# A transformer block on one core: the seam between attention and MLP is put in another order (first MLP unit, last output product, row preparation, one load)

## The chip, the core and the metric

The kernel runs on one core of a Trainium2 chip. The core has five engines with an instruction queue each, worked off in order: TensorE (PE in the profile; its weight loads are PEld), VectorE (DVE), ScalarE (ACT), GpSimd (POOL) and SyncE (SP, which here only issues DMAs; ACT and POOL issue DMAs too). An instruction waits on semaphores for what other engines or DMAs must have finished first. The metric is the time of one execution on the device, in microseconds (us).

## The reference

A pre-norm transformer block over 2048 rows of 576 numbers, 32 heads of 18, then a gated MLP of width 4608:

```python
def _layernorm(x, axis=-1, eps=1e-5):
    m = jnp.mean(x, axis=axis, keepdims=True)
    v = jnp.var(x, axis=axis, keepdims=True)
    return (x - m) / jnp.sqrt(v + eps)
...
    x = A_x
    h = x + _A_ref(_layernorm(x, axis=-1), A_wqkv, A_wo)
    h2 = h + _B_ref(_layernorm(h, axis=-1), B_w_gate, B_w_up, B_w_down)
    return h2
```

`_A_ref` is softmax attention followed by the product with wo (the output product); `_B_ref` is `(gelu(h @ w_gate) * (h @ w_up)) @ w_down`. Inputs and output are f32.

## The kernel before

**Rows and stages.** The 2048 rows are four blocks of 512 (`NB = 4`), each of four tiles of 128 rows (`TPB = 4`). The residual stream lies in `nat`, 16 tiles of 128 x 576. The program is one long list per engine, written out by Python generators: a *main* generator emits the TensorE work piece by piece, and at each of its `yield`s one step of a *side* generator is emitted (`beside`, `take`). So the order on every engine is the order in which the Python code runs; nothing reorders it later.

**Attention, then the output product.** The last head group's attention ends with `out_block` (L593 to L641): it normalizes 128 x 512 numbers and writes them with small DMAs into `XT` (tile name X), the transposed operand of the output product. For the last block, four of these DMAs are issued from ScalarE's queue (L637, L639). `wo_block(b)` (L681) computes the output product of a block: 8 halves of a row tile, 14 matmuls each (L694, shown as L279), each evacuated by VectorE with the residual added (L695), then row statistics (L699) and, at the end, 13 small VectorE operations for the inverse deviation (`rstd_of`, L700). The residual tiles are fetched from x into two buffers (L685).

**The MLP.** The blocks are taken in two pairs (p = 0: blocks 0 and 1, p = 1: blocks 2 and 3), and each pair's 2 x 2 block product is done with 7 products in place of 8, after the scheme of Strassen and Winograd, in f16 high and low parts. So the rows of a pair must first be normalized, combined (T1 to T4), split into high and low parts and transposed: that is `pair_rows` (L713). `rows0()` does it for pair 0 inside the last attention stage, `rows1()` for pair 1. Per row tile (4 of them): two norms on VectorE (L723, L724, shown as L215), four GpSimd subtractions (L726 to L729), three casts on ScalarE (`high`, shown as L732), nine VectorE operations for the low parts (L734 to L736), and five DMA transposes (L749): the one for pieces 9 to 17 is issued on ScalarE's queue, the other four on SyncE's.

**A unit and a down product.** `unit(c, p)` (L895) is one chunk of 256 MLP columns for one pair: 14 products of 7 matmuls (L909), one per `yield`, numbered 1 to 14 below. Banks are shared between products, so a product waits until ScalarE or VectorE has read what its bank held: product 11 adds to the bank that the copy at L955 reads after product 9, product 12 to the one that L959 reads after product 10. Gates are `gate` (L917), casts `high(i, j)` (L920), low parts `low(i, j)` on GpSimd (L923). `down(p)` (L986) is 16 groups of 12 matmuls (L998, shown as L279) that read those high and low parts; VectorE adds each to `nat` (L999). The steady state from L1113 on takes, per two chunks, `unit(c, 1)`, `unit(c+1, 1)`, `down(1)`, `unit(c+2, 0)`, `unit(c+3, 0)`, `down(0)`; the side steps load and split the next weights (`split_matrix`, `split_down`). Both need the largest magnitude of a weight matrix: VectorE reduces it (L127, L131), TensorE transposes the result (L136), VectorE makes a scale of it (L140 to L171), ScalarE then cuts the high parts (L825, L881, L885).

**The seam** (L1073 to L1112). After the last attention step: 8 products of `unit(0, 0)`, with two steps of `out_block` among them (after 2 and after 5 products); then `wo_block(3)`; then products 9 to 14 of `unit(0, 0)`; then `unit(1, 0)`; then `down(0)`, with two side steps per group; then what is left of the side steps; then `load_matrix(w_gate, 2)` on SyncE's queue, and the steady state begins with `unit(0, 1)`, the first unit that reads pair 1's rows.

Of the kernel before, what the change touches and what calls it, by code (L numbers as in the profile page):

```python
# [11 lines left out]
F16 = mybir.dt.float16  # L12
# [6 lines left out]
P = 128  # L19
# [12 lines left out]
def tile_block(  # L32
# [645 lines left out]
    xbs = [view(A, MAT, (D,)), view(WK, 19968, (D,))]  # L678
    PIECES = 2 * NK + 9

    def wo_block(b, ring_):  # L681

        def fetch(t):
            if t < (b + 1) * TPB:
                nc.sync.dma_start(xbs[t % 2], xv[:, t])  # L685

        fetch(b * TPB)
        fetch(b * TPB + 1)
        yield
# [23 lines left out]
    def pair_rows(p, F, T4, parts, high):  # L713

        b12, B22, B11, B21, T1, T2, T3 = (F[:, i] for i in range(7))
        y2, y1 = (F.rearrange("p a b -> p (a b)")[:, i * D : (i + 1) * D] for i in range(2))
        M2, M3 = 2 * P, 3 * P
        for rows in parts:
            nc.gpsimd.memset(rows[:, :, M3 - KR : M3], 0.0)
        jobs = ((0, 4, F[:, 1:5]), (4, 6, F[:, 5:7]), (6, 7, T4.unsqueeze(1)))  # L720
        for i in range(TPB):
            t1, t2 = 2 * p * TPB + i, (2 * p + 1) * TPB + i
            normed(y1, nat[:, t1], t1)  # L723
            normed(y2, nat[:, t2], t2)  # L724
            yield
            nc.gpsimd.tensor_sub(T1, b12, B11)  # L726
            nc.gpsimd.tensor_sub(T2, B22, T1)
            nc.gpsimd.tensor_sub(T4, B21, T2)
            nc.gpsimd.tensor_sub(T3, B22, b12)  # L729
            yield  # L730
            for (o0, o1, f), r in zip(jobs, parts):
                high(r[:, :, :HALF], f)  # L732
                yield
                nc.vector.tensor_sub(r[:, :, M3:], f[:, :, :M2], r[:, :, :M2])  # L734
                nc.vector.tensor_sub(r[:, :, HALF : HALF + KR], f[:, :, M2:], r[:, :, M2:HALF])
                nc.vector.tensor_copy(r[:, :, HALF + KR : HALF + 2 * KR], r[:, :, M2:HALF])  # L736
                k0, k1 = 5 * o0, 5 * o1
                flat = r.rearrange("p a b -> p (a b)")
                for a, b in ((0, 9), (9, 18), (18, 35)):
                    a, b = max(a, k0), min(b, k1)  # L740
                    if a >= b:
                        continue
                    if a < 18:
                        o = (2 * p + a // 9) * TB + i * P
                        dst = XT[:, a % 9 : a % 9 + b - a, o : o + P]
                    else:
                        v = p * PIECES + a - 18
                        dst = VP[:, v : v + b - a, i * P : (i + 1) * P]
                    (turn_on[a % 2] if p else nc.sync).dma_start_transpose(dst, flat[:, (a - k0) * P : (b - k0) * P])  # L749
                yield  # L750


# [3 lines left out]
    def rows0():  # L756
# [2 lines left out]
            view(V, o + 8064 + 1280 * a, (n, 5 * P), F16) for a, n in ((0, 4), (4, 2), (6, 1))],  # L759
            nc.vector.tensor_copy)  # L760

    def rows1():
        return pair_rows(1, view(A, MAT, (7, HALF)), T4s, [
            view(A, MAT + 8064, (4, 5 * P), F16), view(V, 36864, (2, 5 * P), F16),
            view(A, MAT + 8064 + 5120, (1, 5 * P), F16)], nc.scalar.copy)


    S1, S2, S3, S4, A12, A22, A11, A21 = range(8)
    B22, B11, B21, T1, T2, T3, T4 = range(7)
# [125 lines left out]
    def unit(c, p):  # L895

        gsc, hsc = scales[c % 2]
        hh, hl = hts[c % 2]
        g, u = ([b[:, :TB] for b in banks[3 * i : 3 * i + 3]] for i in range(2))

        def product(m, bank, a, b, start):
            wh, wl = slots[c % 2][m]
            ks = [piece(p, 5 * b + k) for k in range(5)]
            mm = []
            for k in range(2):
                mm += [(wh[:, a, k], ks[k]), (wh[:, a, k], ks[3 + k]), (wl[:, a, k], ks[k])]
            mm += [(wh[:, a, 2], ks[2])]
            for i, (w, x_) in enumerate(mm):
                nc.tensor.matmul(bank, w, x_, start=start and i == 0,  # L909
                                 stop=i == len(mm) - 1,  # L910
                                 skip_group_check=not start)

        def gelu(dst, src_):
            nc.scalar.activation(dst, src_, AF.Gelu_apprx_tanh, scale=gsc)

        def gate(dst, v):
            nc.vector.scalar_tensor_tensor(dst, v, hsc, dst, op0=ALU.mult, op1=ALU.mult)  # L917

        def high(i, j, v):
            nc.scalar.copy(hh[:, 2 * i + j], v)  # L920

        def low(i, j, v):
            nc.gpsimd.tensor_sub(hl[:, 2 * i + j], v, hh[:, 2 * i + j])  # L923
# [22 lines left out]
        nc.scalar.copy(au, u[0])  # L946
# [8 lines left out]
        nc.scalar.copy(bg, g[0])  # L955
# [12 lines left out]
        yield  # L968
        product(1, u[0], A22, T4, False)
        low(1, 1, bg)  # L970
        gate(ga, u[0])
        yield
        product(0, g[2], S4, B22, False)
        high(1, 0, ga)
        nc.vector.tensor_add(ag, g[2], ag)
        gelu(ag, ag)
        low(1, 0, ga)
        yield
        product(1, u[2], S4, B22, False)
# [50 lines left out]
    for n in range(NS):  # L1030
# [3 lines left out]
        for kt in range(NT):  # L1034
# [33 lines left out]
            if n == NS - 2 and kt == NT // 2:  # L1068
# [12 lines left out]
    tmps += [view(V, 2 * 2 * PIECES * TB, (TB,)), view(WK, 19968, (TB,)), view(W, 33792, (TB,), F32)]  # L1081
# [6 lines left out]
    it = unit(0, 0)  # L1088
    side = chain(second, pause(5), split_matrix(1, 1, None, lambda: load_down(0, nc.gpsimd), 2),
                 pause(5), split_down(0), rows1())  # L1090

    def beside(main, side, n=1, more=0, head=0):

        for i, _ in enumerate(main):
            if i >= head:
                take(side, n + (i % 3 == 2) * more)

    beside(islice(it, 2), side)
    take(ob)
    beside(islice(it, 3), side)  # L1100
    take(ob)
    beside(islice(it, 3), side)
    beside(wo_block(NB - 1, m_ring), side)
    beside(it, side, 1, 1)
    beside(unit(1, 0), side, 1, 1)
    while not dscs:
        take(side)
    beside(down(0, dscs[-1], NCH == 2), side, 2, head=0)
    run(side)
    blank_rows()  # L1110
    load_matrix(w_gate, 2)
    tmps.append(view(A, MAT, (TB,)))  # L1112
    for sc in range(NCH // 2):  # L1113
        c = 2 * sc
# [2 lines left out]
        if not last:  # L1117
# [49 lines left out]
```

## Time and profile before

| what | value |
|---|---|
| median of 3 runs | 2811.88 us (2808.3 to 2812.98) |
| the profiled execution | 2811.68 us, span 2809.9 us |
| granted TensorE clock, mean | 0.989 |
| busy: PE, DVE, ACT, POOL | 94%, 78%, 54%, 24% of the span |
| last attention matmul | 1547 us |
| `unit(0, 1)` starts, ends | 1666.29, 1694.32 us |

All times inside the execution are counted from the start of the span. In a row of the timeline the columns are start, duration, engine, line, operation, output <- input, count of merged instructions, and in brackets the idle time of the engine just before them with what ended it. A matmul's duration includes its pipeline; the step from one start to the next is what it costs. PEclk is the TensorE clock that the throttle granted.

### The profile page before, as it was taken

The page shows a single profiled execution, that of the slowest core. Times are in us where ns is not written, and L with a number is a line of the kernel's source. Part 1 is how long each engine was busy: PE and PEld are TensorE (multiplying, and loading weights), DVE is VectorE, ACT ScalarE, POOL GpSimd, SP SyncE. Part 2 cuts the span into 40 slices and gives each one's busy share as a digit, 9 for nine tenths or more (in the row PEclk, how much of TensorE's full clock was granted, in tenths as well). Part 3 has the DMA queues.
Part 4 walks back from the last instruction along what each step waited for, and adds up shares of the span by engine and source line. Part 5 has one row for each costly group of instructions (what it writes and reads, how often), then busy time and mean ns, then how long its engine had stood idle before and what let it go on. Part 6 is the DMA issues. An engine that isn't in the chain of part 4 may idle for free. (4 is left out here: it accounts for less than half of the span.)

```text
span 2809.9 us, 43719 instructions
## 1 busy us (share of the span) xinstructions
PE 2643.0 (94%) x16665; PEld 1092.9 (39%) x16665; DVE 2179.0 (78%) x3950; ACT 1517.7 (54%) x1872; POOL 688.2 (24%) x833
## 2 busy tenths in 40 slices
PE   7899999999999999999997779999999999999999
PEld 3542222222222222222233445555555555555555
DVE  6379999999999999999979656575757575656563
ACT  5216877777777777777754324343334343333332
POOL 2101432211212122122215233232323222322221
PEclk9999999999999999999999999999999999999999
DMA  8311110000101010010014241010101010101011
GB/s 218 78 49 42 40 40 14 25 23 14 40 12 36 14 40 12 19 31 18 23 29 105 62 76 32 28 44 16 49 21 38 21 45 19 44 21 38 21 57 39
DMA packets 162823, 111.99 MB, mean 40 GB/s; under 512 B 82612, under 2 KB 141620, under 8 KB 162612
## 3 DMA queue, kind: packets, MB, share of 16 engines
q1 hardware_dynamic: 150479, 95.30, 12.3%
q0 software_dynamic: 7296, 12.66, 1.7%
q8 instruction: 130, 2.13, 0.3%
q10 hardware_dynamic: 4837, 1.25, 0.2%
q14 instruction: 81, 0.66, 0.1%
HBM read 74.45 MB, written 14.42 MB: 32 GB/s over the span
## 5 line engine op out<-in xcount | busy, mean ns | idle before, releaser
L535 DVE TENSOR_REDUCE mx<-bank 128x1 f32<-128x512 f32 x2048 | 1264.9, 682 | 30.0 <-PE bank L532 30.0
L581 ACT ACTIVATE WK<-pair 128x1024 f32<-128x1024 f32 x1024 | 991.4, 1021 | 301.2 <-PE pair L579 300.9
L585 PE MATMUL bank<-WK,V 128*32 128x512 f32 x4096 | 548.3, 607 | 0.2 <-ACT nat L599 0.2
L279 PEld LDWEIGHTS <-WK 128*128 128x128 f16 x3456 | 337.5, 98 | 109.6 <-issue 12.2
L909 PEld LDWEIGHTS <-W 128*128 128x128 f16 x2394 | 234.7, 98 | 284.5 <-issue 7.8
L532 PE MATMUL bank<-W 54*128 54x512 f16 x1024 | 291.4, 382 | 40.1 <-DVE mx L535 10.0
L532 PE MATMUL bank<-A 54*128 54x512 f16 x1024 | 279.8, 380 | 38.1 <-DVE mx L535 6.3
L585 PEld LDWEIGHTS bank<-WK,V 128*32 128x32 f32 x4096 | 81.0, 108 | 438.0 <-issue 410.5
L279 PE MATMUL bank<-W,WK 128*128 128x288 f16 x1728 | 236.6, 286 | 13.1 <-POOL WK L923 7.3
L279 PE MATMUL more<-W,WK 128*128 128x288 f16 x1728 | 235.2, 286 | 4.9 <-DVE nat L999 4.9
L608 POOL TENSOR_TENSOR rp<-rc,minus_one 128x16 f32<-128x16 f32 x28 | 81.8, 2922 | 615.1 <-DMA rc<-nat 615.1
L909 PE MATMUL more<-X,W 128*128 128x512 f16 x792 | 223.8, 379 | 0.0
L909 PE MATMUL more<-V,W 128*128 128x512 f16 x720 | 203.4, 380 | 1.7 <-ACT tmp L959 1.7
L809 POOL TENSOR_TENSOR A<-A 128x384 f32<-128x384 f32 x144 | 146.5, 1038 | 207.9 <-DMA A<-in_B_w_up_dram 119.8
L923 POOL TENSOR_TENSOR WK<-tmp,WK 128x512 f16<-128x512 f32 x73 | 89.9, 1231 | 332.9 <-ACT WK L920 324.5
L579 PE MATMUL pair<-W 56*128 56x512 f16 x1024 | 156.5, 378 | 3.6 <-ACT WK L581 2.8
L825 ACT ACTIVATE W<-A,p_s_m 128x768 f16<-128x768 f32 (+1 forms) x78 | 78.2, 1035 | 147.6 <-DVE p_s_m L171 147.4
L532 PEld LDWEIGHTS <-W 54*128 54x128 f16 x1024 | 59.7, 93 | 248.7 <-issue 220.3
L579 PE MATMUL pair<-A 56*128 56x512 f16 x1024 | 153.7, 375 | 0.2
L532 PEld LDWEIGHTS <-A 54*128 54x128 f16 x1024 | 57.2, 93 | 235.0 <-issue 204.1
L999 DVE SCALAR_TENSOR_TENSOR nat<-more,p_dsc,nat 128x288 f32<-128x288 f32 x144 | 74.4, 517 | 91.1 <-PE more L279 89.6
L927 ACT COPY tmp<-bank 128x512 f32<-128x512 f32 x36 | 20.9, 582 | 214.3 <-PE bank L909 190.6
(262 smaller groups left out, 2884.3 us busy)
## 6 DMA issues: line engine op xcount, KB each, us to landing
A<-in_B_w_down_dram SPq DMA_DIRECT2D x8, 1152.0 KB
nat<-rc SPq DMA_DIRECT2D x32, 256.0 KB
A<-in_B_w_gate_dram SPq DMA_DIRECT2D x64, 128.0 KB
A<-in_B_w_up_dram SPq DMA_DIRECT2D x64, 128.0 KB
qk_hi<-qk SPq DMA_DIRECT2D x36, 128.0 KB
qk_lo<-qk SPq DMA_DIRECT2D x36, 128.0 KB
out_dram<-nat SPq DMA_DIRECT2D x16, 288.0 KB
X<-nat SPq DMA_DIRECT2D x100, 36.0 KB
```

What stands on the lines that cost most here:

```text
L279: nc.tensor.matmul(dst, a, b, start=(i == 0), stop=(i == len(pairs) - 1))
L532: nc.tensor.matmul(pms[j][:, :TB], Q[r, q0 : q0 + P], K[r, kc * TB : (kc + 1) * TB], start=True, stop=True)
L535: nc.vector.tensor_reduce(mx[:, t, 2 * pr + j, kc : kc + 1], pms[j][:, :TB], axis=AX.X, op=ALU.max)
L579: nc.tensor.matmul(pS[:, j, :TB], K[r, kt * P : (kt + 1) * P], Q[r, qc * TB : (qc + 1) * TB], start=True, stop=True)
L581: nc.scalar.activation(pes[(2 * kt + pr) % NPE], pS[:, :, :TB], AF.Exp, scale=ex_reg)
L585: nc.tensor.matmul(acc[32 * hh : 32 * hh + 32, :TB], Vg[n // NB][:, kt * G4 + hh * VC : kt * G4 + hh * VC + 32], pes[(2 * kt + hh // 2) % ...
L608: nc.gpsimd.tensor_tensor(rc, den, minus_one.to_broadcast([P, R]), op=ALU.pow)
L809: op(W8[:, d], W8[:, a], W8[:, b])
L825: by = hi_on or (lambda dst, src, k: nc.scalar.activation(dst, src, AF.Copy, scale=k))
L909: nc.tensor.matmul(bank, w, x_, start=start and i == 0, stop=i == len(mm) - 1, skip_group_check=not start)
L923: nc.gpsimd.tensor_sub(hl[:, 2 * i + j], v, hh[:, 2 * i + j])
L999: nc.vector.scalar_tensor_tensor(nat[:, t, ws], pt[:, :HALF], dsc, nat[:, t, ws], op0=ALU.mult, op1=ALU.add)
```

## The change

1. `unit(0, 0)` runs whole (14 products) ahead of `wo_block(3)`, with the second step of `out_block` after 8 products in place of 5. The last output product takes its banks from the ring of four (`down_ring`) in place of two, and fetches its residual tiles into two buffers of the WK region; the two first fetches are issued before `unit(0, 0)`.
2. `rows1()` is written out anew: its two norms go from VectorE to ScalarE (`nc.scalar.activation` with Identity, scale and bias), and a row tile takes 5 or 4 side steps in place of 8. Its operations on GpSimd, its casts, its low parts and its five DMA transposes stay as they were, in the same order (`turn_rows` holds what was written in `pair_rows`).
3. The extra side steps (`more`, and two per group in `down(0)`) are gone: one side step per yield everywhere. One of the pauses is shorter by one.
4. `blank_rows()` and `load_matrix(w_gate, 2)` become the last side step (`first_load`), so SyncE issues them behind the last DMA transpose, inside `down(0)` rather than behind it. In the first `unit(0, 1)` the side steps begin after 7 products (`head=7`).
5. In every unit, `high(1, 0)` and `low(1, 0)` are emitted ahead of the yield between products 12 and 13, so ahead of that yield's side step; before they stood behind it.

```diff
-    def wo_block(b, ring_):
+    def wo_block(b, ring_, xbs=xbs):
...
     def rows1():
-        return pair_rows(1, view(A, MAT, (7, HALF)), T4s, [
-            view(A, MAT + 8064, (4, 5 * P), F16), view(V, 36864, (2, 5 * P), F16),
-            view(A, MAT + 8064 + 5120, (1, 5 * P), F16)], nc.scalar.copy)
...
+        def high(k):
+            nc.scalar.copy(parts[k][:, :, :HALF], jobs[k][2])
+
+        def low(k, i):
+            o0, o1, f = jobs[k]
+            r = parts[k]
+            nc.vector.tensor_sub(r[:, :, M3:], f[:, :, :M2], r[:, :, :M2])
+            nc.vector.tensor_sub(r[:, :, HALF : HALF + KR], f[:, :, M2:], r[:, :, M2:HALF])
+            nc.vector.tensor_copy(r[:, :, HALF + KR : HALF + 2 * KR], r[:, :, M2:HALF])
+            turn_rows(1, i, 5 * o0, 5 * o1, r)
+
+        for i in range(TPB):
+            t1, t2 = 2 * TPB + i, 3 * TPB + i
+            for y, t in ((y1, t1), (y2, t2)):
+                nc.scalar.activation(y, nat[:, t], AF.Identity, scale=rs[:, t : t + 1],
+                                     bias=nb[:, t : t + 1])
+            nc.gpsimd.tensor_sub(T1, b12, B11)
+            nc.gpsimd.tensor_sub(T2, B22, T1)
+            nc.gpsimd.tensor_sub(T4, B21, T2)
+            nc.gpsimd.tensor_sub(T3, B22, b12)
+            yield
+            high(0)
+            yield
+            low(0, i)
+            high(1)
+            high(2)
+            yield
+            low(1, i)
+            yield
+            low(2, i)
+            if i % 2 == 0:
+                yield
...
         gate(ga, u[0])
+        high(1, 0, ga)
+        low(1, 0, ga)
         yield
         product(0, g[2], S4, B22, False)
-        high(1, 0, ga)
         nc.vector.tensor_add(ag, g[2], ag)
         gelu(ag, ag)
-        low(1, 0, ga)
...
+    last_wo = wo_block(NB - 1, down_ring, [view(WK, 8192 + 4 * D * i, (D,)) for i in range(2)])
+    next(last_wo)
+
+    def first_load():
+        blank_rows()
+        load_matrix(w_gate, 2)
+        yield
+
     side = chain(second, pause(5), split_matrix(1, 1, None, lambda: load_down(0, nc.gpsimd), 2),
-                 pause(5), split_down(0), rows1())
+                 pause(4), split_down(0), rows1(), first_load())
...
-    beside(islice(it, 3), side)
+    beside(islice(it, 6), side)
     take(ob)
-    beside(islice(it, 3), side)
-    beside(wo_block(NB - 1, m_ring), side)
-    beside(it, side, 1, 1)
-    beside(unit(1, 0), side, 1, 1)
-    while not dscs:
-        take(side)
-    beside(down(0, dscs[-1], NCH == 2), side, 2, head=0)
+    beside(it, side)
+    beside(last_wo, side)
+    tmps[5] = view(W, 33792, (TB,), F32)
+    beside(unit(1, 0), side)
+    assert dscs
+    beside(down(0, dscs[-1], NCH == 2), side)
     run(side)
-    blank_rows()
-    load_matrix(w_gate, 2)
...
-        beside(unit(c, 1), side)
+        beside(unit(c, 1), side, head=0 if sc else 7)
```

ScalarE's queue at the seam, before, from the first cast of `unit(0, 0)` on (L639 are the four small DMAs of the last attention output; L946 is the copy behind product 6, L955 and L959 those behind products 9 and 10, L825 the cut of the weights for `unit(1, 0)`):

```order
L920 CAST WK<-tmp 128x512
L625 CAST nat<-nat 128x512
L639 DMA X<-nat 10x512
L639 DMA X<-nat 18x512 x3
L946 COPY V<-more_12734 128x512
L825 ACTIVATE W<-A,p_s_m_12964 128x1152
L825 ACTIVATE W<-A,p_s_m_12964 128x768 x2
L955 COPY WK<-bank_66 128x512
L959 COPY W<-more_12734 128x512
```

The same place now (L962 is the cast, L988, L997 and L1001 the three copies, L956 a gelu):

```order
L962 CAST WK<-tmp 128x512
L988 COPY V<-more_12734 128x512
L625 CAST nat<-nat 128x512
L639 DMA X<-nat 10x512
L639 DMA X<-nat 18x512 x3
L997 COPY WK<-bank_66 128x512
L1001 COPY WK<-more_12734 128x512
L956 ACTIVATE WK<-WK,p_gsc_12143 128x512
```

The copy behind product 6 now stands ahead of the four DMA issues; the copies behind products 9 and 10, which products 11 and 12 wait for, stand right behind them.

ScalarE's queue in `unit(1, 0)`, before, from the copy behind product 6 to the first gelu behind product 10 (L732 are casts of the rows of pair 1, L749 the DMA transpose):

```order
L946 COPY WK<-more_12734 128x512
L732 CAST A<-A 128x4x288
L955 COPY W<-bank_66 128x512
L749 DMA_TRANSPOSE X<-A 128x9x128
L732 CAST V<-A 128x2x288
L959 COPY tmp<-more_12734 128x512
L914 ACTIVATE W<-W,p_gsc_12803 128x512
```

Now, from the copy behind product 9 to the first DMA transpose (L791 are the norms of the first row tile, L778 its first cast):

```order
L997 COPY W<-bank_66 128x512
L1001 COPY tmp<-more_12734 128x512
L956 ACTIVATE W<-W,p_gsc_12805 128x512
L791 ACTIVATE A<-nat,nb,rs 128x576 x2
L956 ACTIVATE tmp<-bank_66,p_gsc_12805 128x512
L962 CAST WK<-W 128x512
L778 CAST A<-A 128x4x288
L962 CAST WK<-tmp 128x512
L763 DMA_TRANSPOSE X<-A 128x9x128
```

The rows of pair 1 begin later in the unit (behind product 10 in place of product 6), and no cast or transpose of theirs stands ahead of the copies behind products 9 and 10 any more.

ScalarE's queue at the end of `unit(1, 1)`, the last unit ahead of a `down(1)`, before (L825 is the cut of the next weights, the cast of tmp behind it is `high(1, 0)`):

```order
L920 CAST WK<-A 128x512
L825 ACTIVATE W<-A,p_s_m_13858 128x1152
L920 CAST WK<-tmp 128x512
L914 ACTIVATE WK<-WK,p_gsc_12803 128x512
L825 ACTIVATE W<-A,p_s_m_13858 128x768
```

And now:

```order
L962 CAST WK<-A 128x512
L962 CAST WK<-tmp 128x512
L867 ACTIVATE W<-A,p_s_m_13860 128x1152
L956 ACTIVATE WK<-WK,p_gsc_12805 128x512
L867 ACTIVATE W<-A,p_s_m_13860 128x768
```

The two have changed places, in each of the eight `unit(c+1, 1)` that have a weight to cut; no other row of ScalarE's queue differs from there to the end.

More of the change, by code (lines that the diff above doesn't have):

```diff
@@ L736, in pair_rows @@
                 nc.vector.tensor_copy(r[:, :, HALF + KR : HALF + 2 * KR], r[:, :, M2:HALF])
[L737 to L749, printed above, removed]
+                turn_rows(p, i, 5 * o0, 5 * o1, r)
                 yield
@@ L760, in rows0, with turn_rows @@
             nc.vector.tensor_copy)
-    def rows1():
-        return pair_rows(1, view(A, MAT, (7, HALF)), T4s, [
-            view(A, MAT + 8064, (4, 5 * P), F16), view(V, 36864, (2, 5 * P), F16),
-            view(A, MAT + 8064 + 5120, (1, 5 * P), F16)], nc.scalar.copy)
+    def turn_rows(p, i, k0, k1, rows):
+        flat = rows.rearrange("p a b -> p (a b)")
+        for a, b in ((0, 9), (9, 18), (18, 35)):
+            a, b = max(a, k0), min(b, k1)
+            if a >= b:
+                continue
+            if a < 18:
+                o = (2 * p + a // 9) * TB + i * P
+                dst = XT[:, a % 9 : a % 9 + b - a, o : o + P]
+            else:
+                v = p * PIECES + a - 18
+                dst = VP[:, v : v + b - a, i * P : (i + 1) * P]
+            (turn_on[a % 2] if p else nc.sync).dma_start_transpose(dst, flat[:, (a - k0) * P : (b - k0) * P])
@@ new lines, in rows1 @@
+    def rows1():
+        F, T4 = view(A, MAT, (7, HALF)), T4s
+        parts = [view(A, MAT + 8064, (4, 5 * P), F16), view(V, 36864, (2, 5 * P), F16),
+                 view(A, MAT + 8064 + 5120, (1, 5 * P), F16)]
+        b12, B22, B11, B21, T1, T2, T3 = (F[:, i] for i in range(7))
+        y2, y1 = (F.rearrange("p a b -> p (a b)")[:, i * D : (i + 1) * D] for i in range(2))
+        M2, M3 = 2 * P, 3 * P
+        for rows in parts:
+            nc.gpsimd.memset(rows[:, :, M3 - KR : M3], 0.0)
+        jobs = ((0, 4, F[:, 1:5]), (4, 6, F[:, 5:7]), (6, 7, T4.unsqueeze(1)))
+        def high(k):
[28 more added lines that the diff above has]
+                yield
@@ L1080, in tile_block @@
     tmps += [small.tile([P, TB], F32, tag="tmp", name="tmp", bufs=3) for _ in range(3)]
-    tmps += [view(V, 2 * 2 * PIECES * TB, (TB,)), view(WK, 19968, (TB,)), view(W, 33792, (TB,), F32)]
+    tmps += [view(V, 2 * 2 * PIECES * TB, (TB,)), view(WK, 19968, (TB,)), view(WK, 8192 + 8 * D, (TB,))]
     pairs_in.close()
@@ L1087, in tile_block, with beside @@
     down_ring = ring([singles[0], more[0], singles[1], more[1]])
-    it = unit(0, 0)
+    last_wo = wo_block(NB - 1, down_ring, [view(WK, 8192 + 4 * D * i, (D,)) for i in range(2)])
[4 more added lines that the diff above has]
+        yield
     side = chain(second, pause(5), split_matrix(1, 1, None, lambda: load_down(0, nc.gpsimd), 2),
-                 pause(5), split_down(0), rows1())
-    def beside(main, side, n=1, more=0, head=0):
+                 pause(4), split_down(0), rows1(), first_load())
+    def beside(main, side, n=1, head=0):
         for i, _ in enumerate(main):
             if i >= head:
-                take(side, n + (i % 3 == 2) * more)
+                take(side, n)
+    it = unit(0, 0)
     beside(islice(it, 2), side)
     take(ob)
-    beside(islice(it, 3), side)
+    beside(islice(it, 6), side)
     take(ob)
-    beside(islice(it, 3), side)
-    beside(wo_block(NB - 1, m_ring), side)
-    beside(it, side, 1, 1)
-    beside(unit(1, 0), side, 1, 1)
-    while not dscs:
-        take(side)
-    beside(down(0, dscs[-1], NCH == 2), side, 2, head=0)
+    beside(it, side)
[4 more added lines that the diff above has]
+    beside(down(0, dscs[-1], NCH == 2), side)
     run(side)
-    blank_rows()
-    load_matrix(w_gate, 2)
     tmps.append(view(A, MAT, (TB,)))
```

## The prediction

> **What bounds the kernel now.** I read the page first: TensorE is busy almost throughout, and the slices with gaps are the first two and those just behind the last attention stage, where the change works.
>
> ```profile
> span 2809.9 us, 43719 instructions
> PE   7899999999999999999997779999999999999999
> ```
>
> A slice is 70 us; the three sevens (from 1475 us on) are the seam. So the question is when TensorE can go on there. I next read its timeline from 1547 us on, in brackets what it waited for. L909 are unit products, L279 the output product up to 1588 us and the down product from 1630 us, L136 transposes of a magnitude.
>
> ```profile
> 1559.97 1.27 PE L279 MATMUL bank<-W,X 128*128 128x288 f16 x9
> 1568.25 0.90 PE L279 MATMUL bank<-W,X 128*128 128x288 f16 x3 [7.01 <-DMA X<-nat]
> 1571.82 0.64 PE L279 MATMUL bank<-W,X 128*128 128x288 f16 x2 [2.67 <-DMA X<-nat]
> ...
> 1577.84 1.88 PE L279 MATMUL more<-W,X 128*128 128x288 f16 x14
> 1579.55 1.88 PE L279 MATMUL bank<-W,X 128*128 128x288 f16 x14
> ...
> 1599.02 1.67 PE L909 MATMUL bank<-X,W 128*128 128x512 f16 x7
> ...
> 1605.91 0.43 PE L136 MATMUL more<-id,am_dn 128*128 128x128 f32 x2 [3.70 <-DVE am_dn L131]
> ...
> 1621.09 3.15 PE L909 MATMUL bank<-V,W 128*128 128x512 f16 x7 [2.66 <-ACT W L955]
> ...
> 1630.49 1.63 PE L279 MATMUL bank<-W,WK 128*128 128x288 f16 x12
> 1631.96 1.63 PE L279 MATMUL more<-W,WK 128*128 128x288 f16 x12
> ...
> 1666.29 1.67 PE L909 MATMUL bank<-X,A 128*128 128x512 f16 x7
> ...
> 1678.71 0.32 PE L136 MATMUL bank<-id,am_m 128*128 128x128 f32 x1 [4.71 <-DVE am_m L131]
> ```
>
> The seam has four stages: output product and rest of `unit(0, 0)`, 1559.97 to 1599.02 (39.05 us); `unit(1, 0)` to 1630.49 (31.47); `down(0)` to 1666.29 (35.80); `unit(0, 1)` to 1694.32. Each holds waits. The chain of waits behind the last one gives product 6 to 8 and the end of that unit, by its 14th product:
>
> ```profile
> 1679.04 2.85 PE more L909 x7
> 1681.88 1.86 PE bank L909 x7
> 1683.75 1.51 PE more L909 x7
> ...
> 1692.81 1.51 PE more L909 x7
> ```
>
> A product costs 1.51 us, and the first two behind a long wait cost 2.85 + 1.86, so 1.7 us more (slow clock). A half of the output product costs 1579.55 - 1577.84 = 1.71 us. What paces the rows of pair 1 is the chain of their DMA transposes (ACTq and SPq are the two issuing queues):
>
> ```profile
> 1656.76 2.71 DMA V<-A
> ...
> 1659.61 3.24 DMA X<-A
> ...
> 1663.00 1.30 SPq L749
> ...
> 1667.15 1.34 SPq L749
> ...
> 1673.52 3.87 DMA A<-in_B_w_gate_dram
> ```
>
> Per row tile ScalarE's transpose lands 3.24 us behind its issue, only then SyncE's four go out, and only when the last of those has landed (2.71 us) does ScalarE issue the next tile's. SyncE's four of the last tile were issued from 1663.00 to 1667.15, so 4.15 us apart; a tile cannot take less than 3.3 + 4.15 + 2.71, some 10.3 us with the hand-overs. ScalarE's four issues stood at:
>
> ```profile
> 1623.33 1.38 ACTq L749 DMA_TRANSPOSE X<-A  x1
> ...
> 1637.95 1.32 ACTq L749 DMA_TRANSPOSE X<-A  x1
> ...
> 1649.23 1.31 ACTq L749 DMA_TRANSPOSE X<-A  x1
> ```
>
> So the tiles took 14.6, 11.3 and 10.4 us (to 1659.61). `unit(0, 1)` started 3.3 us behind SyncE's 1663.00, when that transpose can have landed. It is the chain, not TensorE, that sets its start.
>
> **Part 1: the whole unit ahead of the output product.** Products 9 and 10 now start at 1559.97 and end at 1563.0. Product 11 waits for ScalarE's copy behind product 9, and that still stands behind the four DMA issues:
>
> ```profile
> 1566.13 3.89 ACTq L639 DMA_DIRECT2D X<-nat  x4
> 1570.06 0.58 ACT L946 COPY V<-more 128x512 f32<-128x512 f32 x1 [4.68 <-DMA X<-nat]
> ```
>
> So product 11 starts at 1570.64, 7.7 us later: only two of the six products fill the gap. Products 11 and 12 at the slow clock (4.7), 13 and 14 (3.0): 1578.4. By then X has landed (1571.82 before), the residual tiles too, since their fetches go out before `unit(0, 0)`; the fetches could delay the small DMAs of the normalization on SyncE's queue, which no row prices; I take 0 and keep 1 us for the range. Then 8 halves of 1.71 and a transpose: `unit(1, 0)` starts at 1592.3, 32.3 us in place of 39.05. **Gain 6.7.** The four banks keep VectorE's lag off TensorE.
>
> **Part 2: `unit(1, 0)`.** The waits at 1621 and 1626, for ScalarE copies behind casts of rows, go, as the order shows. The one for the down matrix's magnitude stays in part. I let VectorE end the last half's evacuation and statistics at 1594.4, 2 us behind TensorE; then come the small operations, then two reductions:
>
> ```profile
> 1591.53 0.17 DVE L201 TENSOR_SCALAR ln_v<-mv 128x4 f32<-128x4 f32 x1
> ...
> 1593.92 0.16 DVE L211 SCALAR_TENSOR_TENSOR nb<-mv,rs 128x4 f32<-128x4 f32 x1
> ```
>
> ```profile
> L734 DVE TENSOR_TENSOR A<-A 128x1024 f16<-128x1024 f32 x4 | 5.8, 1461 | 6.5 <-ACT A L732 6.5
> L732 ACT CAST A<-A 128x1152 f16<-128x1152 f32 x4 | 4.6, 1151 | 13.2 <-DMA X<-A 5.1 <-POOL A L727 4.4 <-POOL A L726 3.6
> L726 POOL TENSOR_TENSOR A<-A 128x288 f32<-128x288 f32 x4 | 3.2, 792 | 15.4 <-DVE A L215 15.4
> L127 DVE TENSOR_REDUCE ac_dn<-A 128x1 f32<-128x1152 f32 x2 | 2.7, 1349 | 2.8 <-DMA A<-in_B_w_down_dram 2.8
> L885 ACT ACTIVATE W<-A,p_s_dn 128x576 f16<-128x576 f32 x3 | 2.3, 763 | 0.0
> ```
>
> 1594.4 + 2.5 + 2 x 1.35 + 0.2 = 1599.9, against product 4's end at 1592.3 + 4 x 1.51 = 1598.3: a wait of 1.6 us. The unit takes 14 x 1.51 + 1.6 + 0.2 = 23.0 and ends at 1615.3, in place of 31.47. **Gain 8.4.** A rule of the Trainium skill ("TensorE: Matmul & The Clock Gate", Part 1, on the two states) says that the clock halves only after an idle window of about 3.4 us. Here the row at 1621.09 took 3.15 us for seven matmuls after 2.66 us of wait, so the trace is stricter. By the rule the sum stands; by that row the 1.6 us wait may cost another 1.6.
>
> **Part 3: rows of pair 1 and `down(0)`.** Product 10 ends at 1599.9 + 0.2 + 6 x 1.51 = 1609.2. On ScalarE follow a copy and a gelu (1.4 in all: 0.58 as L946's copy, the gelu of as many columns a little more), two norms (no such row on ScalarE; bounds are L946's 0.58 for 512 columns and L885's 0.76 for 576; I take 0.75 each: 1612.0), a gelu and a cast (1.3), while GpSimd makes T1 (0.79); then the first cast (1.15: 1614.5) and VectorE's low part (1.46 + 0.5). The first transpose is issued at 1616.4, in place of 1623.33. The tile period now: norms on ScalarE stand right behind the last casts instead of behind VectorE's evacuations, ScalarE's work for a tile (1.3 + 0.7 + 0.4 + 1.5 + 1.15 = 5.1, with the issue) fits in 10.3, and the first tile's delay of 14.6 had ScalarE and VectorE busy with the unit's end. I take 10.7, between the floor of 10.3 and the 11.3 seen. The last tile's transpose is issued at 1616.4 + 3 x 10.7 = 1648.5; SyncE's first 3.4 later, landed 3.3 behind that: `unit(0, 1)` starts at 1655.1. TensorE's own work ends near 1640 (16 x 1.47, the step from 1630.49 to 1631.96, from 1615.3, and a wait of 1.2 us for `low(1, 0)`, which GpSimd now does behind the first tile's four subtractions); evacuations queued on VectorE behind the low parts hold the last groups to some 1646, an estimate by the tile period. All of that is covered by the chain. The stage takes 39.8 in place of 35.80. **Loss 4.0**, of a start 15.1 us earlier.
>
> **Part 4: the load ahead, `unit(0, 1)`.** SyncE's last transpose is issued at 1648.5 + 3.4 + 4.15 = 1656.0; eight load issues follow in some 5 us (before, 1668.6 to 1673.52), landed 3.87 later, near 1666.3. VectorE needs them behind product 7 or 8, at 1655.1 + 1.7 + 7 x 1.51 = 1667.4 at the earliest: the wait of 4.71 and its slow clock go. A slow start behind the chain's wait (1.7) comes. 21.1 + 1.7 + 0.2 = 23.0, in place of 28.03. **Gain 5.0.**
>
> **Part 5: `high(1, 0)` ahead of the side step.** One row of the waits from 1700 us on, and the place behind it:
>
> ```profile
> PE bank L279 <- POOL WK L923: 7.3, 8, 0.9
> ```
>
> ```profile
> 1712.67 0.75 DVE L917 SCALAR_TENSOR_TENSOR tmp<-more,p_hsc,tmp 128x512 f32<-128x512 f32 x1 [0.91 <-PE more L909]
> ...
> 1714.47 1.25 ACT L825 ACTIVATE W<-A,p_s_m 128x1152 f16<-128x1152 f32 x1 [2.05 <-DVE p_s_m L171]
> ...
> 1716.31 1.48 POOL L923 TENSOR_TENSOR WK<-tmp,WK 128x512 f16<-128x512 f32 x1 [2.57 <-ACT WK L920]
> ...
> 1717.84 1.22 PEld L279 LDWEIGHTS <-WK 128*128 128x128 f16 x11 [1.22 <-POOL WK L923]
> ```
>
> The gate is done at 1713.4. Now the cast follows at once (0.6), the low part is done at 1715.6, and TensorE needs it at 1716.9: 1.3 us to spare. L825 is released at 1714.47, behind the cast's end at 1714.1, so it loses nothing. **Gain 7.3**, 8 x 0.91; no other wait of TensorE stands in that stretch.
>
> **Sum.** 6.7 + 8.4 - 4.0 + 5.0 = 16.1, and 7.3: 23.4 off the profiled execution's 2811.68 (0.2 below the median of 2811.88): 2788.3, say 2788.
>
> **Rivals.**
> - *The transposes are as slow as before.* If the tiles take 14.6, 11.3 and 10.4 again, `unit(0, 1)` starts 36.3 - 32.1 = 4.2 later: 2792.5. For it: the DMAs are the same. Against: the first tile's 14.6 had other causes. Chance 0.14.
> - *The transposes do not pace.* If ScalarE's and SyncE's could overlap, the start would be TensorE's own 1640: 15 us less and no slow start, 2771.5. Against: 2.71 and 3.24 us of hand-over in the chain, every tile. The Trainium skill ("DMA: Bandwidth & Descriptors", Rules for kernel authors) asks that transposes from two queues be made to wait for each other; by that rule the hand-over is meant and stays, and the trace agrees with its 2.71 us. Chance 0.03.
> - *Part 5 does nothing.* If GpSimd's queue, not the cast's place, were last: 2795.6. Against: GpSimd idle 2.57 ahead of that row. Chance 0.05.
> - *Slower.* ScalarE now holds norms, casts and the transpose issue of a tile in one in-order queue; when an issue waits for landed transposes, the next norms stand behind it, and GpSimd and VectorE behind those. Each us on the period counts three times. To undo 23.4 and add 0.2% (5.6 us; less cannot be told from no change), the period would have to be 20.4 (10.7 + 29 / 3), where the worst seen was 14.6. Its price at 20.4: 2817. Chance 0.02; about no change, at 18 to 20: 0.03.
>
> **Numbers.** My forecast, 2784 to 2792 with 2788 likeliest, has 0.73. The unknowns: period 10.3 to 11.3 (-1.2 to +1.8), the first issue +-2, the 1.6 and the 1 us above. The range 2782 to 2797 takes in the first rival and the third. Faster 0.95, the same 0.03, slower 0.02.
>
> **What would show it.** In the changed profile: a wait of 7 to 8 us ahead of product 11 for ScalarE; `unit(1, 0)` in about 23 us; ScalarE's four transpose issues 10 to 11 us apart, from about 1616; TensorE waiting some 9 us or more ahead of `unit(0, 1)` for X; no wait for am_m in it; no row of TensorE waiting for POOL WK. Wrong would be a start of `unit(0, 1)` before 1650 or behind 1660, or the eight 0.91 still there.

## The result, and the profile after

The changed kernel takes 2787.93 us (median of 4 runs, 2786.91 to 2790.99) against 2811.51 for the kernel before (4 runs beside it): a ratio of 0.9919, 95% interval 0.9902 to 0.9937. That is 23.6 us faster. The profiled execution took 2788.19 us, its span 2786.3. The page of the changed kernel, the same two lines as before:

```profile
span 2786.3 us, 43719 instructions
PE   6899999999999999999997879999999999999999
```

The digits alone hardly differ: a slice is 70 us, so 23 us are a third of one digit's width. The timeline of TensorE shows more. L951 are the unit products now, L279 output and down products as before, L136 the transposes of a magnitude:

```profile
1545.43 1.67 PE L951 MATMUL bank<-X,A 128*128 128x512 f16 x7 [0.75 <-DVE nat L695]
...
1567.26 3.15 PE L951 MATMUL bank<-V,A 128*128 128x512 f16 x7 [6.56 <-ACT WK L997]
...
1589.14 1.67 PE L951 MATMUL bank<-X,W 128*128 128x512 f16 x7
...
1596.48 0.43 PE L136 MATMUL more<-id,am_dn 128*128 128x128 f32 x2 [1.14 <-DVE am_dn L131]
...
1611.85 1.51 PE L279 MATMUL bank<-W,WK 128*128 128x288 f16 x11
1615.42 0.30 PE L279 MATMUL bank<-W,WK 128*128 128x288 f16 x1 [2.06 <-POOL WK L965]
1615.55 2.91 PE L279 MATMUL more<-W,WK 128*128 128x288 f16 x12
1618.26 2.07 PE L279 MATMUL bank<-W,WK 128*128 128x288 f16 x12
...
1654.26 3.15 PE L951 MATMUL bank<-X,A 128*128 128x512 f16 x7 [7.65 <-issue]
...
1660.15 1.68 PE L951 MATMUL bank<-X,A 128*128 128x512 f16 x7
...
1675.26 0.27 PE L136 MATMUL bank<-id,am_m 128*128 128x128 f32 x1
```

The reader is to see the new shape: one wait of 6.56 us ahead of product 11 in place of the two for X; a `unit(1, 0)` of 22.7 us with a single wait of 1.14; a `down(0)` that begins 18.6 us earlier; and a wait of 7.65 us at its end. The profile names no releaser for that last wait ("issue"); the transposes below show what it was. The row at 1660.15 is the third product of `unit(0, 1)`, the one at 1675.26 the transpose of the magnitude, behind product 12 and without a wait. The chain of waits gives the first, second, third and 14th product of `unit(0, 1)`:

```profile
1654.26 3.15 PE bank L951 x7
1657.40 2.91 PE more L951 x7
1660.31 1.51 PE bank L951 x7
...
1677.04 1.51 PE more L951 x7
```

So that unit ends at 1678.55. What TensorE waited for from 1546 us to the end, in us, times, longest:

```profile
PE bank L951 <- issue: 7.6, 1, 7.6
PE bank L951 <- ACT WK L997: 6.6, 1, 6.6
PE bank L279 <- DVE nat L1041: 4.4, 2, 2.3
PE more L279 <- DVE nat L1041: 2.2, 1, 2.2
PE bank L279 <- POOL WK L965: 2.1, 1, 2.1
PE more L136 <- DVE am_dn L131: 1.1, 1, 1.1
```

The eight waits for POOL WK in the steady state are gone; the one left is in the seam. `am_m` is no longer waited for.

**By stages.** Each stage runs from the start of its first row in the timeline to the start of the next stage's first row, `unit(0, 1)` to the end of its 14th product in the chain of waits; so what lies ahead of the seam drops out:

| from, to | before | after | change | forecast |
|---|---|---|---|---|
| `unit(0, 0)` starts | 1547.89 | 1545.43 | -2.46 | 0 |
| `unit(0, 0)` and last output product | 51.13 | 43.71 | -7.42 | -6.7 |
| `unit(1, 0)` | 31.47 | 22.71 | -8.76 | -8.4 |
| `down(0)` and the wait behind it | 35.80 | 42.41 | +6.61 | +4.0 |
| `unit(0, 1)` | 28.03 | 24.29 | -3.74 | -5.0 |
| from there to the end of the span | 1115.58 | 1107.75 | -7.83 | -7.3 |

The sum of the last five rows is 21.1 us, the span fell by 23.6. The other 2.46 lie ahead of `unit(0, 0)`, where no engine's instructions were changed. Over all twelve profiled executions shown here `unit(0, 0)` started between 1544.6 and 1551.0 us. That is scatter of the executions, and 2.46 of the profiled gain belong to it.

### The profile page after: what moved, and what is told of

It reads as the page before. It is cut to its first block, busy times and chain, and to the rows that moved or that the text cites. A ratio compares the mean times of both kernels' runs of the same rounds, so it can differ in the third digit from the quotient of the medians.

```text
span 2786.3 us, 43719 instructions
## 1 busy us (share of the span) xinstructions
PE 2637.7 (95%) x16665; PEld 1094.1 (39%) x16665; DVE 2172.0 (78%) x3942; ACT 1524.9 (55%) x1880; POOL 686.9 (25%) x833
## 3 DMA queue, kind: packets, MB, share of 16 engines
q10 hardware_dynamic: 4837, 1.25, 0.2%
## 4 chain that ended last, share of the span: by engine, by line
PE 48%; DVE 45%; DMA 2%; ACT 1%; issue 1%; ACTq 0%; POOL 0%; DVEq 0%; SPq 0%; POOLq 0%
DVE mx L535 42%; PE bank L951 13%; PE more L951 13%; PE bank L279 9%; PE more L279 7%; PE pair L279 4%; PE bank L532 1%; PE bank L585 1%; DMA nat<-rc 0%; DMA V<-A 0%; DVE st L186 0%; DVE V L734 0%; DMA A<-qk_hi 0%; DMA X<-A 0%; DVE nat L695 0%
## 5 line engine op out<-in xcount | busy, mean ns | idle before, releaser
L279 PEld LDWEIGHTS <-WK 128*128 128x128 f16 x3456 | 338.7, 98 | 98.8 <-issue 7.2
L951 PEld LDWEIGHTS <-W 128*128 128x128 f16 x2394 | 234.9, 98 | 279.2 <-issue 2.4
L532 PE MATMUL bank<-W 54*128 54x512 f16 x1024 | 291.1, 381 | 40.4 <-DVE mx L535 10.1
L279 PE MATMUL bank<-W,WK 128*128 128x288 f16 x1728 | 235.8, 286 | 6.5 <-DVE nat L1041 4.4
L279 PE MATMUL more<-W,WK 128*128 128x288 f16 x1728 | 236.5, 287 | 2.2 <-DVE nat L1041 2.2
L951 PE MATMUL more<-X,W 128*128 128x512 f16 x792 | 224.9, 381 | 0.0
L951 PE MATMUL more<-V,W 128*128 128x512 f16 x720 | 202.9, 380 | 0.0
```

The lines of the kernel that those rows point to most:

```text
L279: nc.tensor.matmul(dst, a, b, start=(i == 0), stop=(i == len(pairs) - 1))
L532: nc.tensor.matmul(pms[j][:, :TB], Q[r, q0 : q0 + P], K[r, kc * TB : (kc + 1) * TB], start=True, stop=True)
L951: nc.tensor.matmul(bank, w, x_, start=start and i == 0, stop=i == len(mm) - 1, skip_group_check=not start)
```

## The experiments

All kernels below ran beside the kernel before, 4 to 6 runs each; medians are given with the ratio to it. "The stages" are the table's: first stage, `unit(1, 0)`, `down(0)`.

**Part 5 alone.** Into the kernel before, only:

```diff
         gate(ga, u[0])
+        high(1, 0, ga)
+        low(1, 0, ga)
         yield
         product(0, g[2], S4, B22, False)
-        high(1, 0, ga)
         nc.vector.tensor_add(ag, g[2], ag)
         gelu(ag, ag)
-        low(1, 0, ga)
```

> The kernel before with part 5 alone: the cast and the low part of (1, 0) ahead of the side step. My theory: the eight waits of TensorE for POOL WK go, 8 x 0.91 = 7.3 us, to about 2804; in the seam it changes nothing. Rival (GpSimd's queue, not the cast's place, was last): 2811, the eight waits still there.

Measured: 2802.65 us, 0.9965 (0.9953 to 0.9977). The eight waits are gone from its trace, `down(0)` takes 35.2 us as before. 9.1 us less, with 7.3 inside the interval (6.5 to 13.2). In its trace the stretch behind `unit(0, 1)` is 8.9 us shorter than before. That the seam stays as it was is not so stage by stage: the first stage took 1.6 us less and `unit(1, 0)` 2.7 more, which nearly cancel. The theory holds for the eight waits; where the 1.6 us beyond 7.3 in that stretch come from isn't settled.

**All transposes of pair 1 on one queue.** In the changed kernel:

```diff
-            (turn_on[a % 2] if p else nc.sync).dma_start_transpose(dst, flat[:, (a - k0) * P : (b - k0) * P])
+            nc.sync.dma_start_transpose(dst, flat[:, (a - k0) * P : (b - k0) * P])
```

> The changed kernel with all five DMA transposes of a row tile of pair 1 on SyncE's queue, so that no transpose waits for one on another queue to land. My theory (the chain of transposes with its two hand-overs paces the start of unit(0, 1)): the tile period falls from 10.5 to some 8.6 us (third transpose landed at 5.5, cast 1.15, low part 1.9), and the last tile's first transpose lands 3.4 us sooner; the start comes 8 to 10 us sooner, as far as the down product's own end allows, to 2778 to 2781. Rival (norms, casts and low parts pace the tiles): period stays above 10, about 2785 (3.4 us).

Measured: 2779.29 us, 0.9881 (0.9865 to 0.9896), so 8.6 us below the changed kernel's 2787.93. First, ScalarE's four transpose issues of the changed kernel, and SyncE's first of its last tile:

```profile
1614.38 1.38 ACTq L763 DMA_TRANSPOSE X<-A  x1
...
1626.58 1.32 ACTq L763 DMA_TRANSPOSE X<-A  x1
...
1637.13 1.31 ACTq L763 DMA_TRANSPOSE X<-A  x1
...
1647.63 1.29 ACTq L763 DMA_TRANSPOSE X<-A  x1
```

```profile
1650.96 1.30 SPq L763 DMA_TRANSPOSE X<-A  x1
```

In the chain of waits of the changed kernel, the landings that the next issue on ScalarE's queue waited for:

```profile
1622.17 4.31 DMA V<-A
1626.58 1.32 ACTq L763
...
1634.26 2.77 DMA V<-A
1637.13 1.31 ACTq L763
...
1644.76 2.73 DMA V<-A
1647.63 1.29 ACTq L763
```

The tiles took 12.2, 10.55 and 10.5 us, each ended by a landing, and `unit(0, 1)` started 3.3 us behind SyncE's 1650.96, as it did before the change. Now the kernel with one queue, the issues of the two X transposes of each tile and TensorE's start:

```profile
1619.87 2.98 SPq L763 DMA_TRANSPOSE X<-A  x2
...
1629.95 2.71 SPq L763 DMA_TRANSPOSE X<-A  x2
...
1637.55 2.68 SPq L763 DMA_TRANSPOSE X<-A  x2
...
1645.41 2.73 SPq L763 DMA_TRANSPOSE X<-A  x2
```

```profile
1648.78 2.80 PE L951 MATMUL bank<-X,A 128*128 128x512 f16 x7 [2.99 <-DMA X<-A]
```

Tiles of 10.1, 7.6 and 7.9 us, and a `down(0)` stage of 31.4 us in place of 42.4. By stages this execution gains 12.0 us, 1.0 of it in `unit(0, 1)`, and it began `unit(0, 0)` 5.55 us later; the medians give 8.6. The same norms, casts and low parts fit into 8 us a tile, so they did not pace it: the hand-over between two queues did. The Trainium skill ("DMA: Bandwidth & Descriptors", Rules for kernel authors) asks for that wait when transposes come from two queues; the trace shows two such landings of some 3 us in each tile, and on one queue, without them, tiles 2.6 to 2.9 us shorter. What is left there is a chain through ScalarE and VectorE: a transpose lands (3.61 us), the next tile's cast (1.16) and low part (1.23 and two short operations) follow.

**The norms on VectorE again.** In the changed kernel's `rows1`:

```diff
-                nc.scalar.activation(y, nat[:, t], AF.Identity, scale=rs[:, t : t + 1],
-                                     bias=nb[:, t : t + 1])
+                normed(y, nat[:, t], t)
```

> The changed kernel with the two norms of pair 1's rows on VectorE again. My theory: a tile of the chain has 5 us of slack on ScalarE, the transposes pace it, so the norm's engine matters only ahead of the first transpose, by 1 us either way: 2787 to 2789. Rival (the norms on ScalarE are what made the tiles short): tiles of 11.3 to 14.6 us again, 2791 or more.

Measured: 2788.88 us, 0.9921 (0.9908 to 0.9935), no difference that can be told from the changed kernel. The first and last transposes issued by ScalarE:

```profile
1615.77 1.38 ACTq L763 DMA_TRANSPOSE X<-A  x1
...
1649.69 1.30 ACTq L763 DMA_TRANSPOSE X<-A  x1
```

33.9 us for three tiles, against 33.25 in the changed kernel and 32.6 to 33.4 in the other kernels below that keep two queues and ScalarE's norms. The first issue comes 0.95 us later behind the start of `unit(0, 0)` (69.90 in place of 68.95), as the theory allowed. The rival is out: of the 3 us by which three tiles became shorter than before (36.3 us), 2.4 are there with the norms on VectorE too.

**Part 1 undone.** In the changed kernel:

```diff
-    last_wo = wo_block(NB - 1, down_ring, [...])
+    last_wo = wo_block(NB - 1, m_ring, [...])
...
-    beside(islice(it, 6), side)
+    beside(islice(it, 3), side)
     take(ob)
-    beside(it, side)
+    beside(islice(it, 3), side)
     beside(last_wo, side)
+    beside(it, side)
```

> The changed kernel with part 1 undone: six products of unit(0, 0) behind the last output product again, which takes its two banks again; the residual tiles stay fetched early. My theory: all of the seam behind it shifts by what part 1 gave, 7 us, to about 2795. Rival (the new wait ahead of product 11 has taken the place of the one for X): no more than 3 us lost, 2788 to 2791.

Measured: 2796.67 us, 0.994 (0.9927 to 0.9954), 8.7 us above the changed kernel. The first stage is 50.8 us in place of 43.7, the next two stay (22.8, 41.8). The first of its two waits is the old one:

```profile
1568.57 0.90 PE L279 MATMUL bank<-W,X 128*128 128x288 f16 x3 [5.98 <-DMA X<-nat]
```

So part 1 gave 7.1 us in its own stage, and all behind it moved along.

**The four small DMAs issued from GpSimd.** In the changed kernel's `out_block`:

```diff
-                    other = nc.scalar if n == NS - 1 else nc.sync
+                    other = nc.gpsimd if n == NS - 1 else nc.sync
```

> The changed kernel with the four small DMAs of the last attention output issued from GpSimd's queue rather than ScalarE's. My theory: product 11 no longer waits behind the issues (6.6 us and a slow clock), the unit's six products run while X lands, and the output product starts when X has landed, 5 us sooner; the rest shifts along, to about 2783. Rival (X is last anyway and lands later from GpSimd): 0 to 2 us, 2786 to 2788.

Measured: 2782.43 us, 0.9895 (0.988 to 0.991), 5.5 us below the changed kernel. The first stage is 35.6 us, 8.1 less, the others 23.0 and 42.1. ScalarE's copy and what it held, in the changed kernel:

```profile
1562.69 3.89 ACTq L639 DMA_DIRECT2D X<-nat  x4
1566.62 0.58 ACT L997 COPY WK<-bank 128x512 f32<-128x512 f32 x1 [4.87 <-DMA X<-nat]
```

and product 11 without the issues:

```profile
1566.67 1.67 PE L951 MATMUL bank<-V,A 128*128 128x512 f16 x7 [0.41 <-ACT WK L997]
```

The wait and its slow clock go, and X has landed when the unit is through. On GpSimd's queue the four issues take 2.07 us, and TensorE waits for nothing behind them. Its execution began the unit at 1550.98, the changed kernel's at 1545.43: compared by starts alone, nothing would be seen; by stages it is plain.

**The side steps of `unit(0, 1)` from its first product on, and the load behind `down(0)`.** Two kernels, each an edit of the changed one:

```diff
-        beside(unit(c, 1), side, head=0 if sc else 7)
+        beside(unit(c, 1), side)
```

> The changed kernel with the side steps of the first unit(0, 1) from its first product on. My theory: the loads land near 1665.4 (the last issue 1661.5 and 3.87), the magnitude is ready at 1666.6, TensorE asks for it behind product 5 at 1664.8: a wait of 1.8 us and up to 1.7 of slow clock, 2790 to 2791.5. Rival (the early load hides it): 2788.

```diff
-                 pause(4), split_down(0), rows1(), first_load())
+                 pause(4), split_down(0), rows1())
...
     run(side)
+    blank_rows()
+    load_matrix(w_gate, 2)
```

> The changed kernel with blank_rows and load_matrix(w_gate, 2) behind down(0) again, head 7 kept. My theory as it stands now, against my own part 4: SyncE issues the loads behind the last transpose either way, since nothing else stands between in its queue, so nothing changes: 2788. Rival (the load's place in the program matters, as part 4's heading had it): up to 5 us lost, 2793.

Measured: 2788.39 us, 0.9913 (0.99 to 0.9927), and 2788.71 us, 0.9916 (0.9902 to 0.9929). Neither can be told from the changed kernel by its time. With head 0 the wait is back, small, and `unit(0, 1)` takes 1.2 us longer than in the changed kernel:

```profile
1665.91 0.32 PE L136 MATMUL bank<-id,am_m 128*128 128x128 f32 x1 [1.18 <-DVE am_m L131]
```

With the load put back, SyncE's last transpose and its first load issue:

```profile
1656.87 1.35 SPq L763 DMA_TRANSPOSE V<-A  x1
1658.31 1.39 SPq L837 DMA_DIRECT2D A<-in_B_w_gate_dram  x1
```

The load goes out 1.44 us behind the transpose, as in the kernel before (1667.15 and 1668.58). Its place in the program moves nothing, since SyncE's queue has nothing in between.

**Both edits that gained, and two more.** One queue and GpSimd's issue together:

> Both edits at once: all transposes of pair 1 on SyncE's queue, and the four small DMAs issued from GpSimd. My theory: the two act at different places, the shift ahead of unit(1, 0) and the chain behind it, and add: 8.6 and 5.5 off 2788, about 2774. Rival (what the second saves is eaten by the wait of the first, since TensorE waits for X again ahead of unit(0, 1)): 2777 to 2779.

Measured: 2771.59 us, 0.9853 (0.9838 to 0.9868), 16.3 us below the changed kernel. They add, and a little more. A wait of 2.75 us for the copy behind product 9 was left; with GpSimd's issue alone it had been 0.41 us at the same place of the program. To that kernel:

```diff
-    beside(islice(it, 6), side)
+    beside(islice(it, 7), side)
     take(ob)
```

> The kernel with both edits (one queue, GpSimd issue), and the second step of out_block after 9 products of unit(0, 0) rather than 8, so that ScalarE's copy behind product 9 stands ahead of the cast of the attention output. My theory: the wait of 2.7 us ahead of product 11 and its slow clock (1.3) go, product 12 waits for its own copy at most 1 us; X lands no more than 0.5 us later: 2768 to 2770. Rival (X lands last anyway): 2771.6.

Measured: 2767.87 us, 0.985 (0.983 to 0.9871): the lowest median of all, 20 us below the changed kernel and 44.7 below the one before. The wait at product 11 is gone, product 12 has one of 1.25, where at most 1 was expected, and the first stage is 3.2 us shorter. But the interval overlaps that of the kernel without this edit, and the wait that went had varied from 0.41 to 2.75 us without it, so how much of the 3.7 us is the edit's isn't settled. And to that one, `pause(6)` in place of `pause(4)`:

> The same with the rows of pair 1 begun two side steps later (behind product 12 of unit(1, 0)), so that GpSimd does the low parts of the unit ahead of the first tile's subtractions. My theory (the rows still pace the start of unit(0, 1), where TensorE waits 3.0 us for X): the 2.06 us ahead of the first down group go, but the rows start some 2 us later and the start of unit(0, 1) with them: 1 to 3 us slower than the kernel without this edit, 2770 to 2772. Rival (TensorE's own work paces it): 2 us faster, 2766 to 2768.

Measured: 2773.13 us, 0.9868 (0.9848 to 0.9888). TensorE's start of `unit(0, 1)` in the two, first with `pause(4)`, then with `pause(6)`:

```profile
1636.37 1.02 PE L951 MATMUL bank<-X,A 128*128 128x512 f16 x4 [3.04 <-DMA X<-A]
```

```profile
1635.32 3.03 PE L951 MATMUL bank<-X,A 128*128 128x512 f16 x7 [6.05 <-DMA X<-A]
```

The 2.05 us for GpSimd's low part are gone from the second, and 3 us more of waiting for X stand in their place, as the theory had it. The later start that it forecast isn't there: the first transposes go out 0.9 us later behind the start of `unit(0, 0)`, but the first tile takes 8.6 us in place of 10.1. Counted from the start of `unit(0, 0)`, `unit(0, 1)` starts at 91.24 us with `pause(4)` and at 90.71 with `pause(6)`. By the profile the two are alike; the median is 5.3 us apart, because three of the four runs of the second took 2773 us and the profiled one 2766.84. Why those three were slower isn't settled. The edit gains nothing.

## Why the prediction was right, and where it was not

- **Part 1** (forecast 6.7, in the trace 7.4, undone 7.1): right, with its new wait: 7.7 us foreseen ahead of product 11, 6.56 found, behind the four issues on ScalarE's queue. That those issues were the cause, the GpSimd kernel shows.
- **Part 2** (8.4; 8.8): right. The wait for the down matrix's magnitude was 1.14 us, forecast 1.6, and the product behind it ran at its full 1.51 us. So the extra 1.6 us that the row at 1621.09 would have allowed did not come; the Trainium skill's idle window ("TensorE: Matmul & The Clock Gate", Part 1) agrees with this wait. No kernel undoes this part alone: that the waits went with the casts of rows ahead of the copies is read from the two queues and the traces. The kernel with part 1 undone shows that it doesn't hang on part 1, since there the stage keeps its 22.8 us.
- **Part 3** (loss 4.0; 6.6): the mechanism was right and is shown by the one-queue kernel; the size was off. The first transpose was issued 68.95 us behind the start of `unit(0, 0)`, forecast 68.5. The two norms, for which there had been no row on ScalarE, cost the 0.75 us each that I took: the next instruction started 1.51 us behind the start of the first. The tile period was mis-sized: three tiles took 33.25 us where I took 32.1, all of it in the first tile, whose last transpose needed 4.31 us to land where later ones needed 2.7. What fell on that landing the DMA queues of the changed kernel show, from 1624.38 to 1627 us (packets, MB, share of the DMA engines):

```profile
q8 instruction: 1, 0.02, 2.3%
q1 hardware_dynamic: 4, 0.00, 0.2%
```

  All but four packets of the round's transposes had started by then. One load of instructions (the program's own code, on a queue of its own) ran from 1624.42 to 1625.40, and the last two packets started at 1625.39; of the 16 counts that make a landing 15 came by 1624.87, the last at 1626.48. In the four executions where such a load fell at the end of the first round, the first tile took 12.1 to 12.2 us; in the two where it fell in the middle (part 1 undone, GpSimd's issue), 11.6. So the late landing is put down to that load by its times alone; no run moved it.

  Of the 2.6 us by which the loss was larger, these tiles make 1.1 (33.25 less 32.1), the later first issue 0.4, and the other 1.1 are no loss of time: the two stages ahead gained 0.7 and 0.4 more than forecast, so the wait for X, whose end the transposes set, began that much sooner.
- **Part 4** (5.0; 3.7): the gain came, but not for the reason in its heading, the load ahead. The loads went out right behind the last transpose (at 1656.58, when `unit(0, 1)` had begun), as in the kernel before and as the working itself has it, and putting them back cost nothing. What counted was when TensorE asks for the magnitude. The working had VectorE need the loads behind product 7 or 8; with `head=7` TensorE came to the magnitude only behind product 12, at 1675.26. With side steps from the first product on, it was asked for behind product 5, as before, and a wait of 1.18 us came back where 4.71 had been. Of that difference 2.7 us are the slow start behind the long wait, which puts product 5 that much later, and 0.8 a magnitude ready that much sooner behind the unit's start. The term that was mis-sized is the slow start: priced at 1.7 us, it cost 2.9 (1654.26 to 1660.15 for two products, 3.02 at full speed), nearly all of what the gain lacks.
- **Part 5** (7.3; 7.8): right, and shown alone (8.9 us in that stretch of its own trace).
- **The total** (23.4; 23.6 by the medians): closer than the parts deserve. In the profiled pair the parts make 21.1, and the 2.5 us missing came from scatter ahead of the seam. That the total came out within 0.2 us is luck.
- **The signs.** Three were off: the wait ahead of product 11 (6.56 us, forecast 7 to 8), ScalarE's first two issues (12.2 us apart, forecast 10 to 11) and the wait ahead of `unit(0, 1)` (7.65 us, forecast some 9 or more). And one row of TensorE still waits for POOL WK, in the seam: 2.06 us for `low(1, 0)`, which the working had at 1.2.
- **The rivals.** That the transposes don't pace falls with the one-queue kernel. That they are as slow as before is half true for the first tile. That part 5 does nothing falls. The slower case (a longer period because norms, casts and issues share ScalarE's queue) found nothing for it: with the norms back on VectorE the tiles took no less time.

## What to carry to other kernels

When transposes issued from two queues have to wait for each other, count the landings per round; here two of some 3 us each paced a whole stage, and one queue was 8.6 us faster than two. A DMA issue on a compute engine's queue costs the work behind it: four issues held two small copies and those copies held TensorE, and on the queue of an engine with nothing urgent behind them they held nobody. Moving a load or a step ahead in the program moves nothing if its queue had nothing in between, so look at the queue's rows before crediting it; and a gain found in one stage by its own start and end survives a scatter that hides it in the total.

## What the runs showed of the hardware that was not expected

- The slow clock behind a wait differs in price: behind 7.65 us the next two products cost 2.9 us more than at full speed; behind 4.71 us in the kernel before, 1.7 more; behind 1.14 us nothing. But behind 2.06 us, in the middle of the down product, the next two groups took 2.71 and 1.91 us from start to start, in place of 1.47. A threshold of one idle window of 3.4 us (the same page of the Trainium skill) would have spared them; in this trace it did not. Yet the same wait of 2.05 us with GpSimd's issue cost nothing, nor did waits of 2.27 and 2.19 us later in the changed kernel's down product. The granted clock shows a pattern behind this: around the seam every stretch at full or half clock is a whole multiple of 3.41 us long, so the clock changes on a grid of such steps, which lies elsewhere in each execution. Below are two steps of the changed kernel, then three of the kernel with GpSimd's issue (from and to; length; busy time of PE, PEld, DVE, ACT, POOL with counts; granted clock; DMA share; GB/s):

```profile
1612.31:1615.73 3.42, 1.36 (x12) 0.86 (x11) 2.59 (x4) 0.00 (x0) 3.05 (x3) 1.00 0.01 1
1615.73:1619.14 3.41, 3.41 (x16) 2.10 (x15) 2.54 (x7) 1.86 (x4) 0.00 (x0) 0.50 0.45 87
```

```profile
1608.50:1611.92 3.42, 2.56 (x17) 1.44 (x15) 3.33 (x4) 0.58 (x2) 3.42 (x4) 1.00 0.00 0
1611.92:1615.33 3.41, 2.22 (x19) 1.78 (x20) 1.81 (x6) 1.63 (x3) 1.14 (x2) 1.00 0.45 87
1615.33:1618.74 3.41, 3.41 (x30) 2.74 (x28) 2.91 (x8) 2.15 (x3) 1.16 (x1) 1.00 0.54 106
```

  In the first the whole wait lies within one step, TensorE is idle for 2.06 us of it, and the next step runs at half clock. In the other the edge of a step cuts the wait into 0.86 and 1.19 us, and the clock stays at 1.00. Over all twelve executions, from 1500 to 1720 us, 625 steps at full clock were followed by another, with 1.96 us idle at most; 49 were followed by one at half clock, with 1.92 us idle at least. So what a wait of some 2 us costs here hangs on how much of it falls into one step. This is a pattern of these traces; no run moved a wait on the grid to test it.
- The executions scatter ahead of the seam: `unit(0, 0)` began between 1544.6 and 1551.0 us in twelve profiled executions whose instructions up to there are the same on TensorE.
